# Expert products in turn: the second product of one expert position beside the first product of the next

## The chip, the cores and the metric

The kernel runs on one core of one Trainium2 chip. The metric is device time in microseconds (us) of one execution. Three timed runs of the kernel before took 490.77, 490.84 and 494.41 us, so the median is 490.84 us.

## The reference

A retention attention (4 batches, 8 heads, 768 positions, head width 64, blocks of 64) makes `x`, 3072 tokens of 512 numbers. Then a mixture of 8 experts is applied to it: each token goes to the one expert with the largest logit.

```
logits = x @ w_gate
e_idx = np.argmax(logits, axis=1)
gate_w = probs[np.arange(N), e_idx]
eom = 1.0 / (1.0 + np.exp(-(x @ w_output_gate)))
for e in range(E):
    mask = e_idx == e
    h = np.maximum(x[mask] @ w1[e], 0.0)
    ye = h @ w2[e]
    out[mask] = gate_w[mask, None] * eom[mask, e, None] * ye
```

`w1[e]` is 512x1024 and `w2[e]` 1024x512, all in 32-bit floating point. The change touches only the loop over the experts, which is the second half of the kernel's time.

## The kernel before

**Positions.** The experts are sorted by how many tokens chose them. Position 0 is the fullest. The capacity `CAP` of the positions is 448, 432, 416, 400, 400, 384, 368 and 368 tokens. Capacity in blocks of 128 rows (`KT`) is 4 for positions 0 to 4 and 3 for 5 to 7. Positions 1 to 4 are `TURNED`: their second product is computed with the output features on the partitions and turned back afterwards. The others, called rows positions here, compute it with the tokens on the partitions.

**One product is three matmuls.** Each 32-bit operand is split into a high and a low part of type fp32r, and `mm3` (L77 to L80) adds high by high (L78), high by low (L79) and low by high (L80) in one PSUM bank.

**The stages of a position.** The first product (`up`, matmuls to the tiles `ph`) runs over 8 feature groups `fc`, each with 4 inner steps, so 8 x 4 x 3 = 96 matmuls. After each `fc`, `up_act` takes the ReLU on ScalarE (`hhi`, L923) and the low part on VectorE (`hlo`, L924). Then the second product runs: for a turned position, `down` makes 4 output groups of 24 matmuls each (`py`), so 96; for a rows position, KT row blocks of 24 matmuls (`pyr`). In the kernel before, all of `up` of a position stands ahead of all of its second product, and that ahead of the next position.

**What runs beside it.** A weight piece of 1 MB is loaded on SyncE's queue (L128, L130) and split by quarters, high part on ScalarE (L143) and low part on VectorE (L152); two pieces of `w1` and two of `w2` per position, in three raw buffers. GpSimd (POOL) gathers the rows of `x` two positions ahead by indirect DMA (L792, 12 to 14 per position), VectorE transposes them (L883) and ScalarE and VectorE split them (L895, L896). After a turned second product, VectorE transposes the bank (`zt`, L985), scales it (`yo`, L991), and POOL scatters the rows to the output by indirect DMA (L1002, 13 or 14 per position). A rows position scales each block (L1063) and scatters it with one DMA (L1066). `down_banks` fills the unused columns of a bank with zeros (L940) where the capacity is no multiple of 32; that is so for positions 1, 3 and 4, and in the kernel before it stands in the middle of `up`.

**What sets the order.** Everything stands under a manual schedule: each engine runs its instructions in the order in which the program text issues them. The main loop of the kernel below fixes the order; buffers come round from pools (8 PSUM banks with the tag `bank`, 45 slots with the tag `slot`), where a new tile waits for the last use of the oldest one.

## Time and profile before

| | before |
|---|---|
| three timed runs | 490.77, 490.84, 494.41 us |
| the profiled execution's own time | 494.69 us |
| its span | 493.0 us |
| mean granted TensorE clock | 0.933 |
| TensorE (PE) busy | 438.5 us (89%) |
| VectorE (DVE) busy | 281.4 us (57%) |
| GpSimd (POOL) busy | 273.9 us (56%) |
| ScalarE (ACT) busy | 200.6 us (41%) |

Times inside the execution are counted from the start of the span. The positions follow the attention and the routing: the second product of position 1 starts at 209.22 us, the first product of position 2 at 228.79, and the last second product ends at 487.88. A PE that is busy is not a PE at its peak: matmuls overlap in the pipeline, so the time from one matmul's start to the next one's, the pitch, says more than the duration of one.

### The profile page before, as it was taken

To read this page: it belongs to the slowest core of one execution; us is meant where nothing else is said; L and a number is where in the kernel's file an instruction comes from. 1 tells how busy PE (TensorE), PEld (TensorE's weight loads), DVE (VectorE), ACT (ScalarE), POOL (GpSimd) and SP (SyncE) were. 2 spreads that over 40 slices of the span, in tenths; PEclk is the share of its full clock that TensorE was granted. 3 is DMA by queue.
4 is the path that set the end of the run, shared out by engine and by line. 5 is a ranking of instruction groups with operands and counts; after the bars stand their busy time and mean duration, and the time that the engine had idled before them with its cause. 6 is when DMAs were issued, how large, how long until landed. Compare 5 with 4: busy or idle time off the path is not lost.

```text
span 493.0 us, 10864 instructions
## 1 busy us (share of the span) xinstructions
PE 438.5 (89%) x4016; PEld 385.1 (78%) x4016; DVE 281.4 (57%) x791; ACT 200.6 (41%) x505; POOL 273.9 (56%) x323
## 2 busy tenths in 40 slices
PE   8999999978699989999549966998799869999995
PEld 5799888866597958889439953998599748898985
DVE  5677776727666266495039621957196248186531
ACT  3688787737332134270125201632171234073410
POOL 5587888676616777637731775076637735601002
PEclk9999999979889999999859995999889959999999
DMA  9999999975312929728105451555527245745001
GB/s 188 214 279 270 261 246 245 235 185 188 98 63 58 208 60 288 170 102 212 55 29 162 163 115 40 121 185 122 129 97 197 70 107 195 186 107 195 19 21 41
DMA packets 85512, 73.04 MB, mean 148 GB/s; under 512 B 58572, under 2 KB 64528, under 8 KB 85456
## 3 DMA queue, kind: packets, MB, share of 16 engines
q1 hardware_dynamic: 76192, 51.58, 41.0%
q0 software_dynamic: 9120, 20.73, 14.6%
q8 instruction: 33, 0.54, 0.5%
q14 instruction: 23, 0.19, 0.1%
q10 hardware_dynamic: 144, 0.00, 0.0%
HBM read 59.27 MB, written 13.41 MB: 147 GB/s over the span
## 4 chain that ended last, share of the span: by engine, by line
PE 78%; issue 9%; DVE 3%; DMA 3%; another core or an unknown queue 2%; SPq 2%; ACT 1%; POOL 0%; POOLq 0%; ACTq 0%; DVEq 0%
PE ph_None L80 9%; PE ph_None L79 9%; PE ph_None L78 9%; PE ps L393 5%; PE py L80 5%; PE py L78 5%; PE py L79 5%; PE pyr L79 4%; PE pyr L78 4%; PE pyr L80 4%; PE po L445 4%; PE po L481 3%; PE pk L341 2%; PE po L428 2%
## 5 line engine op out<-in xcount | busy, mean ns | idle before, releaser
L792 POOL DMA_INDIRECT xg<-x_d,rows x89 | 96.5, 1085 | 89.4 <-issue 35.8
L923 ACT ACTIVATE hhi<-ph_None 128x400 fp32r<-128x400 f32 (+4 forms) x56 | 28.1, 502 | 173.0 <-remote 85.5
L80 PE MATMUL ph_None<-xhi,wlo 128*128 128x400 f32 (+4 forms) x224 | 80.8, 361 | 16.9 <-issue 16.8
L78 PE MATMUL ph_None<-xhi,whi 128*128 128x400 f32 (+4 forms) x224 | 80.5, 359 | 9.3 <-issue 9.1
L79 PE MATMUL ph_None<-xlo,whi 128*128 128x400 f32 (+4 forms) x224 | 81.1, 362 | 6.9 <-issue 6.8
L152 DVE TENSOR_TENSOR wlo<-raw,whi 128x512 fp32r<-128x512 f32 x128 | 84.5, 683 | 3.2 <-ACT whi L143 2.7
L924 DVE SCALAR_TENSOR_TENSOR hlo<-ph_None,hhi 128x400 fp32r<-128x400 f32 (+4 forms) x56 | 31.4, 560 | 93.8 <-issue 64.3
L143 ACT CAST whi<-raw 128x512 fp32r<-128x512 f32 x128 | 74.5, 616 | 2.1 <-DMA raw<-in_moe_w_dram 2.1
L1002 POOL DMA_INDIRECT out_dram<-yo,outrow x53 | 53.3, 1006 | 18.9 <-issue 14.9
L78 PEld LDWEIGHTS ph_None<-xhi,whi 128*128 128x128 f32 x224 | 44.3, 198 | 18.6 <-issue 17.0
L80 PEld LDWEIGHTS ph_None<-xhi,wlo 128*128 128x128 f32 x224 | 44.7, 199 | 17.3 <-issue 16.9
L79 PEld LDWEIGHTS ph_None<-xlo,whi 128*128 128x128 f32 x224 | 44.4, 198 | 12.8 <-issue 12.4
L79 PE MATMUL py<-hlo,whi 128*128 128x400 f32 (+2 forms) x128 | 45.2, 353 | 0.1
L80 PE MATMUL py<-hhi,wlo 128*128 128x400 f32 (+2 forms) x128 | 45.1, 352 | 0.1
L78 PE MATMUL py<-hhi,whi 128*128 128x400 f32 (+2 forms) x128 | 45.1, 352 | 0.0
L403 DVE TENSOR_TENSOR at<-ps,decay 128x512 f32<-128x512 f32 x48 | 31.6, 685 | 23.4 <-PE ps L393 19.7
L1066 POOL DMA_INDIRECT out_dram<-yn,table x12 | 12.2, 1014 | 51.5 <-DVE yn L1063 28.8
L78 PE MATMUL pyr<-whi,hhi 128*128 128x512 f32 (+2 forms) x96 | 38.4, 400 | 1.2 <-ACT hhi L923 1.2
L79 PE MATMUL pyr<-wlo,hhi 128*128 128x512 f32 (+2 forms) x96 | 38.3, 399 | 0.9 <-DVE wlo L152 0.8
L80 PE MATMUL pyr<-whi,hlo 128*128 128x512 f32 (+2 forms) x96 | 38.1, 397 | 0.5 <-issue 0.5
L361 ACT COPY qT<-pq 64x256 f32<-64x256 f32 x88 | 34.4, 391 | 3.3 <-PE pq L341 2.5
L638 POOL DMA_INDIRECT tab_d<-rec,idx x24 | 24.9, 1037 | 17.1 <-issue 15.8
(182 smaller groups left out, 831.5 us busy)
## 6 DMA issues: line engine op xcount, KB each, us to landing
raw<-in_moe_w_dram SPq DMA_DIRECT2D x15, 1024.0 KB
raw<-in_moe_w_dram SPq DMA_DIRECT2D x24, 512.0 KB
qkv<-in_k_dram SPq DMA_DIRECT2D x20, 256.0 KB
qkv<-in_v_dram SPq DMA_DIRECT2D x20, 256.0 KB
qkv<-in_q_dram SPq DMA_DIRECT2D x38, 128.0 KB
x_d<-xn POOLq DMA_DIRECT2D x17, 256.0 KB
raw<-in_moe_w_dram SPq DMA_DIRECT2D x16, 128.0 KB
raw<-in_moe_w_dram POOLq DMA_DIRECT2D x4, 512.0 KB
```

What stands on the lines that cost most here:

```text
L78: nc.tensor.matmul(ps, a[0], b[0], start=first, stop=False)
L79: nc.tensor.matmul(ps, a[0], b[1], start=False, stop=False)
L80: nc.tensor.matmul(ps, a[1], b[0], start=False, stop=last)
L143: nc.scalar.copy(out=hi, in_=src)
L152: eng.tensor_tensor(out=lo, in0=src, in1=hi.bitcast(F32), op=ALU.subtract)
L361: nc.scalar.copy(out=view(qT[0][r]), in_=src)
L403: nc.vector.tensor_tensor(out=at, in0=ps.rearrange("p (g t) -> p g t", g=NPAIR), in1=dec[:, j], op=ALU.mult)
L638: nc.gpsimd.indirect_dma_start(out=tab_d, out_offset=bass.IndirectOffsetOnAxis(ap=idx, axis=0), in_=rec, in_offset=None, bounds_check=P * ...
L792: nc.gpsimd.indirect_dma_start(out=xg[(p, b // 4)][:, (b % 4) * P : (b % 4 + 1) * P], out_offset=None, in_=x_q, in_offset=bass.IndirectOff ...
L923: nc.scalar.activation(out=hi[:, r], in_=ph[:, r], func=AF.Relu)
L924: nc.vector.scalar_tensor_tensor(out=lo[:, r], in0=ph[:, r], scalar=0.0, in1=hi[:, r].bitcast(F32), op0=ALU.max, op1=ALU.subtract,)
L1002: nc.gpsimd.indirect_dma_start(out=out.rearrange("t (q f) -> (t q) f", q=4), out_offset=bass.IndirectOffsetOnAxis(ap=ogs[p][0][:, b : b + ...
```

## The change

The change is in the order of the instructions. The number of matmuls, of DMAs and of bytes is the same.

First, a class `Buffers` hands out banks and slots: the program says itself when a tile is given back (`free`), and the next `take` gets the one given back longest ago. 8 banks are held that way, 13 slots of 32-bit data and 32 of split parts. Second, from position 1 on the loop takes, for each position `p`, its second product in 8 steps, one `fc` each: 4 banks at once, 3 matmuls for each (12 matmuls, 9 in a rows position). Between two steps stand the 12 matmuls of one `fc` of the first product of position `p + 1`. All four banks of the second product are complete only after step 7, and are then turned together (`turn_bank`); scaling and scattering of them (`scale_rows`, `emit_turned`) move into the next turn of the loop, into its groups 0 and 1. Third, the gathers stand three positions ahead of `p`, behind the scatters, and the weight pieces are split in the order in which they are used now, in buffers of their own for each of the two products. Fourth, the zero fill of `down_banks` now stands at the start of a turn, ahead of step 0. Position 7 runs its second product alone.

In the order listings, line numbers are those of the kernel before (L78 to L80) or of the changed one (L101 to L103), and a tile bears the name that its buffer was first taken under: a bank named `ph_0` can hold a second product, and a slot named `xg` scaled rows.

TensorE at the start of the second product of position 1, before:

```order
L79 MATMUL ph_7_None<-xlo_3_3381,whi_3489 128x432
L80 MATMUL ph_7_None<-xhi_3_3380,wlo_3490 128x432
L78 MATMUL py_0_3638<-hhi_0_3549,whi_3553 128x432
L79 MATMUL py_0_3638<-hlo_0_3550,whi_3553 128x432
L80 MATMUL py_0_3638<-hhi_0_3549,wlo_3554 128x432
L78 MATMUL py_0_3638<-hhi_1_3572,whi_3553 128x432
L79 MATMUL py_0_3638<-hlo_1_3573,whi_3553 128x432
L80 MATMUL py_0_3638<-hhi_1_3572,wlo_3554 128x432
```

One bank takes the groups 0 to 7 of `h` in a row. TensorE at the end of step 1 of the same position in the changed kernel, with the first product of position 2 behind it:

```order
L102 MATMUL ph_2_None<-hlo_1_3610,whi_3554 128x432
L103 MATMUL ph_2_None<-hhi_1_3609,wlo_3555 128x432
L101 MATMUL ph_3_None<-hhi_1_3609,whi_3554 128x432
L102 MATMUL ph_3_None<-hlo_1_3610,whi_3554 128x432
L103 MATMUL ph_3_None<-hhi_1_3609,wlo_3555 128x432
L101 MATMUL ph_4_None<-xhi_0_3748,whi_3703 128x416
L102 MATMUL ph_4_None<-xlo_0_3749,whi_3703 128x416
L103 MATMUL ph_4_None<-xhi_0_3748,wlo_3704 128x416
L101 MATMUL ph_4_None<-xhi_1_3752,whi_3703 128x416
```

The rows with 432 columns are the second product of position 1, now with a new bank after every three matmuls; those with 416 columns are the first product of position 2.

VectorE around the zero fill of position 3, before (`hlo` is the low part of h, `wlo` that of a weight quarter):

```order
L924 SCALAR_TENSOR_TENSOR hlo_3_4552<-ph_3_None,hhi_3_4551 128x400
L152 TENSOR_TENSOR wlo_4476<-raw_4335,whi_4475 128x4x4x32
L940 MEMSET py_0_4560 128x16
L940 MEMSET py_1_4562 128x16
L940 MEMSET py_2_4564 128x16
L940 MEMSET py_3_4566 128x16
L924 SCALAR_TENSOR_TENSOR hlo_4_4582<-ph_4_None,hhi_4_4581 128x400
```

The fill stands behind group 3 of the first product, four groups ahead of its use. The same place in the changed kernel, from the turned banks of position 2 on (L1021 is the transpose of a bank, L922 the low part of x of position 4, into slots first named `hlo`):

```order
L1021 STREAM_TRANSPOSE xg_0_3888<-ph_1_None 128x416
L177 TENSOR_TENSOR wlo_4529<-raw_4417,whi_4528 128x512 x2
L922 TENSOR_TENSOR hlo_0_3848<-y_1_4455,hhi_0_3847 128x160
L922 TENSOR_TENSOR hlo_2_3966<-y_1_4455,hhi_2_3965 128x160
L950 SCALAR_TENSOR_TENSOR hlo_6_3778<-ph_6_None,hhi_6_3777 128x400
L177 TENSOR_TENSOR wlo_4529<-raw_4417,whi_4528 128x512 x2
L922 TENSOR_TENSOR hlo_3_4016<-y_1_4455,hhi_3_4015 128x160
L922 TENSOR_TENSOR hlo_1_3610<-y_1_4455,hhi_1_3609 128x160
L950 SCALAR_TENSOR_TENSOR hlo_7_3789<-ph_7_None,hhi_7_3788 128x400
L972 MEMSET ph_2_None 128x16
L972 MEMSET ph_3_None 128x16
L972 MEMSET ph_4_None 128x16
```

The fill now stands behind the low part of group 7, which is the last work of the turn, and its use is the next thing TensorE does.

POOL's indirect DMAs from the gather for position 4 on, before (a gather reads `x_d`, a scatter writes `out`):

```order
L792 DMA xg_0_4217<-x_d,rows_4212 128x128 x4
L792 DMA xg_1_4230<-x_d,rows_4212 128x128 x4
L792 DMA xg_2_4243<-x_d,rows_4212 128x128 x4
L792 DMA xg_3_4256<-x_d,rows_4212 128x128
L1002 DMA out_dram<-yo_0_4295,outrow_4041 12288x128 x4
L1002 DMA out_dram<-yo_1_4297,outrow_4041 12288x128 x4
L1002 DMA out_dram<-yo_2_4299,outrow_4041 12288x128 x4
L1002 DMA out_dram<-yo_3_4301,outrow_4041 12288x128
```

Here 13 gathers stand at the start of the second product of position 2 and its 13 scatters behind them. In the changed kernel, from the scatter of position 2 on:

```order
L1043 DMA out_dram<-xg_1_3635,outrow_4375 12288x128 x4
L1043 DMA out_dram<-xg_0_3622,outrow_4375 12288x128 x4
L1043 DMA out_dram<-yo_0_4203,outrow_4375 12288x128 x4
L1043 DMA out_dram<-yo_1_4205,outrow_4375 12288x128
L817 DMA yo_2_4207<-x_d,rows_4663 128x128 x4
L817 DMA yo_3_4209<-x_d,rows_4663 128x128 x4
L817 DMA xg_3_3927<-x_d,rows_4663 128x128 x4
```

The scatters of position 2 come first and the gathers for position 6 directly behind them, both issued in group 1 of the turn in which the second product of position 3 runs.

The diff, with the removed lines left out (they stand in the kernel above):

```diff
+    class Buffers:
+        def __init__(self, make):
+            self.make, self.count, self.back, self.held = make, None, [], []
+        def hold(self, count):
+            self.count = count
+        def take(self, name, newest=False):
+            if self.count is None:
+                return self.make(name)
+            if len(self.held) < self.count and not (newest and self.back):
+                self.held.append(self.make(name))
+                return self.held[-1]
+            return self.back.pop(-1 if newest else 0)
+        def free(self, t):
+            if any(t is h for h in self.held):
+                self.back.append(t)
+    def slots_of(dtype):
+        return Buffers(lambda name: pool.tile([P, 512], dtype, tag="slot", bufs=NSLOT, name=name))
+    banks = Buffers(lambda name: psum.tile([P, 512], F32, tag="bank", name=name))
+    slots, parts = slots_of(F32), slots_of(F32R)
+    bank, slot, part = banks.take, slots.take, parts.take
...
+            side = 0 if i == len(pieces) - 1 else pieces[i][1]
             wparts[pieces[i]] = (
...
+                wpool.tile([P, 4, 512], F32R, tag=f"whi{side}", bufs=2, name=f"whi_{i}"),
+                wpool.tile([P, 4, 512], F32R, tag=f"wlo{side}", bufs=2, name=f"wlo_{i}"),
             )
...
         nc.vector.transpose(ys[(p, i // 2)][:, 512 * (i % 2) : 512 * (i % 2) + w], xg[(p, i)][:, 0:w])
+        slots.free(xg[(p, i)])
...
+            hts[(p, fc)] = (part(f"hhi_{p}_{fc}"), part(f"hlo_{p}_{fc}"))
...
+        banks.free(ph)
...
+    def down_blocks(p):
+        return list(range(NKC if p in TURNED else KT[p]))
     def down_banks(p):
...
+        for j in down_blocks(p):
+            py = phs[(p, "y", j)] = bank(f"py_{p}_{j}")
+            if p in TURNED and CAP[p] < 32 * NB[p]:
                 nc.vector.memset(py[:, CAP[p] : 32 * NB[p]], 0.0)
...
+    def down(p, fc, js):
+        whi, wlo = wparts[(p, 1, fc // 4)]
+        hi, lo = hts[(p, fc)]
+        for j in js:
+            py = phs[(p, "y", j)]
+            if p in TURNED:
+                sl = slice(j * P, (j + 1) * P)
+                mm3(
+                    py[:, 0 : CAP[p]], (whi[:, fc % 4, sl], wlo[:, fc % 4, sl]),
+                    (hi[:, 0 : CAP[p]], lo[:, 0 : CAP[p]]), fc == 0, fc == NFC - 1,
+                )
+            else:
+                r = slice(j * P, min(j * P + P, CAP[p]))
+                mm3(
+                    py[0 : r.stop - r.start, :], (hi[:, r], lo[:, r]), (whi[:, fc % 4, :], wlo[:, fc % 4, :]),
+                    fc == 0, fc == NFC - 1,
+                )
...
+    zts = {}
+    def turn_bank(p, dc):
         py = phs.pop((p, "y", dc))
...
+        zt = zts[(p, dc)] = slot(f"zt_{p}_{dc}", newest=True)
+        nc.vector.transpose(zt[:, 0 : 32 * NB[p]], py[:, 0 : 32 * NB[p]])
+        banks.free(py)
+    def scale_rows(p, dc):
+        zt, nb = zts.pop((p, dc)), NB[p]
         for k in range(KT[p]):
             if dc == 0:
...
+                yts[(p, k)] = slot(f"yo_{p}_{k}")
             bs = slice(4 * k, min(4 * k + 4, nb))
             n = bs.stop - bs.start
             nc.vector.tensor_tensor(
...
+                out=yts[(p, k)].rearrange("p (b f) -> p b f", b=4)[:, 0:n, 32 * dc : 32 * dc + 32],
                 in0=zt.rearrange("p (b c) -> p b c", c=32)[:, bs],
                 in1=ogs[p][1][:, bs].unsqueeze(2).broadcast_to([P, n, 32]),
                 op=ALU.mult,
             )
+        slots.free(zt)
...
+        order = [4, 5, 6, 8, 7, 9]
+        for p in range(2, E):
+            order += [i for i in (4 * p + 2, 4 * p + 4, 4 * p + 3, 4 * p + 5) if i < len(pieces)]
+        done = [0]
+        def next_split(count):
+            for _ in range(count):
+                i, j = divmod(done[0], 4)
+                if i >= len(order):
+                    return
+                split_quarter(order[i], j)
+                if j == 3 and i + 2 < len(order):
+                    load_piece(order[i + 2], nc.gpsimd if i == 0 else nc.sync)
+                done[0] += 1
+        work = next_x(1)
+        for fc in range(NFC):
+            up(0, fc, 1)
+            if fc >= 4:
+                next_split(1)
+                for f in work[:2]:
+                    f()
+                work = work[2:]
+            if fc == 0:
+                load_rows(2)
+            if fc == 4:
+                row_index(2)
+                gather(2)
+        for j in range(2, KT[0]):
             for fc in range(NFC):
...
+                down_rows_mm(0, j, fc)
+            if j == 2:
+                for f in work:
                     f()
...
+                next_split(4)
+            emit_rows(0, j, phs.pop((0, "y", j)))
+        banks.hold(8)
+        slots.hold(NSLOT - 4 * NPAIR - 2 * NFC)
+        parts.hold(4 * NPAIR + 2 * NFC)
+        load_rows(3)
+        load_rows(4)
+        work = next_x(2)
+        for fc in range(NFC):
+            for kc in range(NKC):
+                up_mm(1, fc, None, kc)
+            if fc > 0:
+                up_act(1, fc - 1, None)
+            next_split(1)
+            if fc == 1:
+                out_index(1)
+            if fc == 2:
+                row_index(3)
+                gather(3)
+            for f in {5: work[0:2], 6: work[2:6], 7: work[6:7]}.get(fc, ()):
+                f()
+        up_act(1, NFC - 1, None)
+        rest = work[7:]
+        for p in range(1, E - 1):
+            nxt = p + 1
+            down_banks(p)
+            js = down_blocks(p)
+            x = next_x(p + 2)
+            last = p - 1
+            old = [lambda d=d: scale_rows(last, d) for d in range(NKC)] if last in TURNED else []
+            tasks = {i: [] for i in range(NFC)}
+            tasks[0] += old[0:2]
+            tasks[1] += old[2:4]
+            tasks[1].append(lambda: row_index(p + 3))
+            if last in TURNED:
+                tasks[1].append(lambda: emit_turned(last))
+            tasks[1].append(lambda: gather(p + 3))
+            tasks[6].append(lambda: load_rows(p + 4))
+            if nxt not in TURNED:
+                tasks[0].append(lambda: load_outs(nxt))
+            if p in TURNED and p > 1:
+                tasks[2].append(lambda: out_index(p))
+            if p == 1:
+                tasks[3].append(count_over)
+            tasks[3] += x[0:2]
+            tasks[4] += x[6:8] + x[2:3]
+            tasks[5] += x[3:6]
+            tasks[6] += x[8:10]
+            tasks[7] += x[10:12]
+            def step(fc):
+                down(p, fc, js)
+                for t in hts.pop((p, fc)):
+                    parts.free(t)
+            step(0)
+            for i in range(NFC):
+                if i < NFC - 1:
+                    step(i + 1)
+                if p == 1 and i == 0:
+                    for f in rest:
+                        f()
+                if i == NFC - 2 and p in TURNED:
+                    for d in range(NKC):
+                        turn_bank(p, d)
+                elif i == NFC - 2:
+                    for j in js:
+                        emit_rows(p, j, phs.pop((p, "y", j)))
+                for kc in range(NKC):
+                    up_mm(nxt, i, None, kc)
+                next_split(2)
+                for f in tasks[i]:
+                    f()
+                up_act(nxt, i, None)
+            for g in range(NPAIR):
+                for t in xts.pop((nxt, g)):
+                    parts.free(t)
+        p = E - 1
+        nc.gpsimd.drain()
+        for j in range(KT[p]):
+            if j == KT[p] - 1:
+                last_rows(p, j)
+                continue
+            for fc in range(NFC):
+                down_rows_mm(p, j, fc)
+            emit_rows(p, j, phs.pop((p, "y", j)))
```

111 lines of the change are left out of this document (9 added, 102 removed).

## The prediction

> **What bounds the kernel now.** I read the page's shares and its chain of waits first, then TensorE's waits, then the windows by stage, and last the instructions of TensorE and POOL one by one where a window came out too long. The page's share of TensorE and its chain:
>
> ```profile
> PE 438.5 (89%) x4016; PEld 385.1 (78%) x4016; DVE 281.4 (57%) x791; ACT 200.6 (41%) x505; POOL 273.9 (56%) x323
> ...
> PE 78%; issue 9%; DVE 3%; DMA 3%; another core or an unknown queue 2%; SPq 2%; ACT 1%; POOL 0%; POOLq 0%; ACTq 0%; DVEq 0%
> ```
>
> TensorE is the path, with 78% of the chain; another 9% is "issue", time for which the profile shows no releaser. The view of TensorE's waits says where:
>
> ```profile
> PE ph_None L80 <- issue: 16.8, 20, 1.6
> PE ph_None L78 <- issue: 9.1, 14, 1.6
> PE ph_None L79 <- issue: 6.8, 14, 1.6
> ```
>
> (Columns: total us, times, longest.) All of it is in the first products, 32.7 us in 48 waits. No such row exists for the second products of the turned positions. The windows by stage, cut where the tile changes; columns are length, then busy time and instructions of PE, PEld, DVE, ACT and POOL, granted clock, DMA share, GB/s:
>
> ```profile
> 209.22:228.79 19.57, 19.32 (x98) 17.98 (x96) 17.03 (x45) 9.27 (x22) 9.76 (x9) 1.00 0.40 134
> 228.79:264.07 35.28, 23.54 (x98) 20.25 (x96) 12.41 (x41) 6.98 (x14) 18.27 (x19) 0.76 0.37 90
> 264.07:282.15 18.08, 18.08 (x98) 17.98 (x96) 15.23 (x43) 7.42 (x18) 10.01 (x10) 1.00 0.47 154
> 282.15:315.68 33.53, 24.89 (x98) 20.02 (x97) 12.17 (x41) 7.50 (x16) 17.29 (x17) 0.75 0.37 90
> 315.68:332.96 17.28, 17.28 (x98) 17.28 (x97) 11.21 (x33) 6.80 (x16) 10.36 (x10) 1.00 0.57 172
> 332.96:358.88 25.92, 20.64 (x98) 18.13 (x98) 12.52 (x44) 6.26 (x13) 15.14 (x16) 0.92 0.51 120
> 377.45:403.41 25.96, 20.42 (x97) 17.66 (x97) 8.52 (x17) 6.00 (x13) 17.33 (x18) 0.85 0.52 124
> 420.99:438.74 17.75, 16.49 (x97) 16.01 (x96) 8.57 (x16) 6.50 (x14) 6.98 (x7) 1.00 0.56 135
> 455.16:471.16 16.00, 16.00 (x98) 16.00 (x97) 9.16 (x15) 6.90 (x14) 0.97 (x1) 1.00 0.05 14
> ```
>
> The rows are the second product of position 1, then first and second products of 2 and of 3, then the first products of 4 to 7. Each is 96 matmuls. Where nothing disturbs, 96 take 18.08 us at 416 columns (a pitch of 0.188), 17.28 at 400 and 16.00 at 368, so about 16.7 at 384 (16.00 x 384 / 368). The first products of positions 2 to 6 take longer by 35.28 - 18.08 = 17.20, 33.53 - 17.28 = 16.25, 25.92 - 17.28 = 8.64, 25.96 - 16.7 = 9.26 and 17.75 - 16.00 = 1.75: together 53.1 us. This is the sum that the change plays for.
>
> **What the stalls look like.** TensorE's instructions in the first product of position 2, and finer windows, in the same columns as above:
>
> ```profile
> 238.13 0.45 PE L78 MATMUL ph_None<-xhi,whi 128*128 128x416 f32 x1
> 239.55 0.35 PE L79 MATMUL ph_None<-xlo,whi 128*128 128x416 f32 x1 [0.97 <-issue]
> 240.97 0.35 PE L80 MATMUL ph_None<-xhi,wlo 128*128 128x416 f32 x1 [1.07 <-issue]
> ```
>
> ```profile
> 172.00:182.00 10.00, 8.87 (x40) 6.04 (x40) 5.42 (x12) 4.07 (x11) 7.54 (x8) 1.00 0.16 46
> 334.40:337.30 2.90, 1.61 (x7) 1.14 (x8) 2.62 (x7) 0.00 (x0) 1.01 (x1) 1.00 0.16 45
> 338.80:350.40 11.60, 11.44 (x64) 11.11 (x62) 6.47 (x29) 3.04 (x6) 9.07 (x9) 1.00 0.61 146
> 228.79:237.65 8.86, 8.86 (x49) 8.80 (x47) 2.68 (x7) 1.02 (x2) 6.72 (x8) 1.00 0.74 164
> 237.65:255.80 18.15, 6.41 (x16) 3.35 (x14) 2.42 (x12) 1.02 (x2) 11.55 (x12) 0.63 0.14 44
> 255.80:264.07 8.27, 8.27 (x36) 8.09 (x36) 7.31 (x22) 4.93 (x10) 0.00 (x0) 0.79 0.48 111
> ```
>
> A matmul that should follow after 0.19 us follows after 1.42, within one bank, with operands long there. The half clock is a result, since it is still 1.00 when the stalls begin, and costs its own part afterwards: 36 matmuls in 8.27 us, a pitch of 0.230. The common mark is POOL. Its rows:
>
> ```profile
> 186.65 1.08 POOL L792 DMA_INDIRECT xg<-x_d,rows  x1 [1.43 <-issue]
> ...
> 206.23 0.95 POOL L1066 DMA_INDIRECT out_dram<-yn,table  x1 [0.31 <-issue]
> ...
> 216.60 1.06 POOL L792 DMA_INDIRECT xg<-x_d,rows  x1 [9.42 <-issue]
> ...
> 251.57 0.98 POOL L1002 DMA_INDIRECT out_dram<-yo,outrow  x1 [0.30 <-issue]
> ...
> 269.39 1.05 POOL L792 DMA_INDIRECT xg<-x_d,rows  x1 [16.84 <-PE py L80]
> ...
> 338.76 1.03 POOL L1002 DMA_INDIRECT out_dram<-yo,outrow  x1 [3.07 <-DVE yo L991]
> ...
> 365.31 1.37 POOL L792 DMA_INDIRECT xg<-x_d,rows  x1 [9.87 <-DVE y L883]
> ...
> 398.98 0.98 POOL L1002 DMA_INDIRECT out_dram<-yo,outrow  x1 [0.30 <-issue]
> ```
>
> From 216.60 to 252.55 POOL issues 28 indirect DMAs, one each 1.3 us: 14 gathers, then 14 scatters. The stall begins at 237.65, 21 us into that run, and ends 3 us after it. From 365.31 to 399.96 it is the same; from 269.39 on 26 follow each other, some 34 us. Where a pause of 3.07 us parts the run, the scatters from 338.76 on go beside a dense TensorE for 11.6 us (64 matmuls in the window). What links POOL to TensorE's sequencer no view shows. I read the rows as: a run of indirect DMAs over some 20 us makes TensorE crawl for its remainder.
>
> **Part by part.** *The order of matmuls.* Their number and shapes stay, so dense time stays. Taking every loss of the first products off the profiled execution's own time gives 494.69 - 53.1 = 441.6 us.
>
> *Four banks open.* The second product needs 4 banks for a whole turn and the first one cycles through the rest. Up_act of a group has the 12 matmuls of the next step as cover, some 2.2 us, against one ReLU and one low part of 0.56 (row below). I take nothing; without cover it would be about 1 us a group.
>
> *The zero fill.* VectorE's groups from 205 us on:
>
> ```profile
> L152 DVE TENSOR_TENSOR wlo<-raw,whi 128x512 fp32r<-128x512 f32 x100 | 66.2, 683 | 0.5 <-ACT whi L143 0.5
> L924 DVE SCALAR_TENSOR_TENSOR hlo<-ph_None,hhi 128x400 fp32r<-128x400 f32 (+4 forms) x52 | 29.0, 557 | 92.2 <-issue 62.7 <-ACT hhi L923 29.4
> L896 DVE TENSOR_TENSOR xlo<-y,xhi 128x256 fp32r<-128x256 f32 (+2 forms) x48 | 15.2, 357 | 0.7 <-ACT xhi L895 0.7
> ...
> L985 DVE STREAM_TRANSPOSE zt<-py 128x416 f32<-128x416 f32 (+1 forms) x16 | 10.0, 622 | 18.4 <-PE py L80 13.1 <-PE ph_None L80 4.7 <-remote 0.5
> ...
> L940 DVE MEMSET py<- 128x16 f32 x8 | 0.2, 72 | 0.0
> ```
>
> At the start of positions 3 and 4, step 0 waits for the fill of its bank, and the fill stands on VectorE behind everything that begins when step 7 of the position before ends: 4 transposes (4 x 0.622), 4 weight parts (4 x 0.683), 4 parts of x (4 x 0.357), 2 low parts (2 x 0.557) and the fill (4 x 0.072), 8.0 us in all. TensorE has 24 matmuls of the first product for it, 24 x 0.18 = 4.3 us. It waits 3.7 us, twice. At position 1 there are no transposes; the last ReLU and low part and the fill come after TensorE's last matmul, some 1.2 us. Sum 8.6 us; its bounds are 0, should VectorE's overlap hide it, and twice that. Who waits behind it: TensorE's whole queue.
>
> *Scales, splits and loads.* The scaling moves one turn on and is waited for by POOL alone. Splits and weight loads keep their number per position; VectorE has 12 to 17 us of work in stages of 17 to 19 us dense, so they fit, though with little to spare. I take nothing.
>
> *POOL.* The gathers for position 3 no longer wait behind the first product of position 1: the gap of 9.42 us before 216.60 goes, and the gathers for position 4 follow. From 186.65 on 13 + 2 + 13 + 13 = 41 DMAs of 1.31 us stand in a row, 53.7 us. After that come 14 scatters and 12 gathers, then twice 13 and 12, and 13 scatters alone: 33.8, 32.5, 32.5 and 16.9 us, each in a turn of some 35 us, so parted by pauses of a few us. Past the 20 us mark lie 33.7 + 13.8 + 12.5 + 12.5 = 72.5 us, nearly all of it gathers now, since the scatters stand first in a run. What a us past the mark costs TensorE beside scatters: 17.20 / 16.0 = 1.08 in the first run, 9.26 / 14.7 = 0.63 in the one from 365.31. Beside gathers: in 334.40 to 337.30 7 matmuls took what 16 could have, 1.64 of 2.90 us, or 0.57; in 172 to 182 the idle time is 1.13 of 10.00, or 0.11. I take 0.4, nearer to the first, whose matmuls have the same shape: 29 us (8 to 41).
>
> *Sum.* 441.6 + 8.6 + 29 = 479.2 us for the profiled execution, which is 3.85 above the median of the runs; by the ratio 490.84 / 494.69 that is 475.5, say 476. With the ends of the gathers' price it is 455 to 487.
>
> **Rivals.** *The stall needs scatters late in a run.* Then nothing is left of it, as scatters now come first: 441.6 + 8.6 = 450.2, or 447 us. For it: 338.80 to 350.40, scatters after a pause and a dense TensorE. Against it: 334.40 to 337.30, a stall with gathers alone.
>
> *The stall goes with the scatters wherever they are.* All 53 of them remain: the loss of 53.1 stays, and the fill adds 0 to 8.6, 491 to 499 us. For it: the long stalls all lie in scatters. Against it: the same dense window.
>
> *Slower: the run's length decides, at the scatters' price.* The place is POOL's queue from 186.65 on; the 72.5 us past the mark cost 0.93 each (42.7 us lost in 45.7 us past the mark, the runs from 216.60, 269.39 and 365.31), 67 us: 441.6 + 8.6 + 67 = 517, or 513. It decides once a us of gathers costs more than (53.1 - 8.6) / 72.5 = 0.61. Against it: both gather rows are below that.
>
> *The clock drops at the bank changes.* If the granted clock fell as in 255.80 to 264.07 (pitch 0.230 for 0.188, 22% more) throughout the changed stages, their dense 245.9 - 53.1 = 192.8 us (209.22 to 455.16) would grow by 42, to 450.2 + 42 = 492, or 489 us. The Trainium skill, page "TensorE: Matmul & The Clock Gate", section "A second HAM failure mode: psum-queue depth-cycling", has such a case: cycling through PSUM banks left small idle gaps between groups of matmuls, and the clock swung between half and full. Against it here: the window from 455.16 changes banks every 12 matmuls with 16.00 of 16.00 us busy and the clock at 1.00; what a change every 3 does no row shows.
>
> **How the numbers follow.** About 1% can be told from no change. Forecast 0.36 (0.05 of it within 1%), no stall left 0.20, stall with the scatters 0.22 (0.12 within 1%, 0.10 slower), long runs 0.16, clock 0.06 (0.04 within 1%, 0.02 faster and slower). Faster 0.52, within 1% 0.21, slower 0.27. The range 445 to 506 leaves out most of the long runs and the lower end of the second case, some 0.2.
>
> **What would show it.** "Issue" in TensorE's waits below 20 us confirms the forecast; above 30 the third or fourth case holds; near 0 the second. Stalls should lie in POOL's gathers and not in scatters. A wait of 2 to 4 us on VectorE's fill should stand at the start of positions 3 and 4. POOL should have a run of over 45 us from about 187 on. The forecast is wrong if stalls start within 5 us of a run's first DMA, if they appear with POOL idle, or if TensorE waits for weight or x parts by more than 5 us in all.

## The result, and the profile after

The changed kernel takes 521.59 us (four runs, 521.34 to 526.49) where the kernel before takes 491.71 (490.77 to 494.41): a ratio of 1.062, with a 95% interval of 1.055 to 1.070. It is slower by some 30 us. The forecast was 476 us, faster than before, and the range 445 to 506. The profiled execution of the kernel before was one of its slower ones (494.69 us), so three or four microseconds between its profile and that of the changed kernel mean nothing.

The page of the changed kernel, its shares and its chain:

```profile
PE 446.8 (86%) x4016; PEld 390.4 (75%) x4016; DVE 279.3 (54%) x791; ACT 199.7 (38%) x505; POOL 275.2 (53%) x323
...
PE 64%; another core or an unknown queue 10%; DVE 7%; issue 7%; DMA 4%; ACT 2%; SPq 2%; POOL 2%; POOLq 0%; DVEq 0%
```

TensorE's share of the chain falls from 78 to 64%; VectorE rises from 3 to 7%, and "another core or an unknown queue" from 2 to 10%. TensorE's waits:

```profile
PE ph_None L101 <- issue: 22.8, 18, 8.8
PE ph_None L102 <- issue: 14.2, 21, 1.7
PE ph_None L103 <- issue: 11.8, 16, 2.3
PE ph_None L101 <- DVE ph_None L972: 4.7, 2, 2.8
```

48.8 us are named "issue", where before had 32.7. Below them stands the zero fill, 4.7 us in two waits, which before did not have. The windows of three turns (one turn: the second product of a position and the first product of the next), cut at the first gap between matmuls (columns as in the prediction):

```profile
278.14:293.75 15.61, 15.61 (x86) 15.56 (x85) 9.44 (x29) 4.90 (x10) 12.26 (x12) 1.00 0.68 183
293.75:315.33 21.58, 9.17 (x20) 5.09 (x20) 1.00 (x3) 0.00 (x0) 14.28 (x15) 0.57 0.14 43
336.05:352.85 16.80, 16.80 (x95) 16.80 (x94) 10.19 (x35) 4.91 (x10) 13.14 (x13) 1.00 0.61 168
352.85:372.04 19.19, 9.84 (x25) 5.61 (x24) 2.81 (x6) 2.44 (x6) 13.23 (x13) 0.64 0.46 102
389.92:406.31 16.39, 16.39 (x94) 16.23 (x94) 10.24 (x35) 4.86 (x10) 12.80 (x12) 1.00 0.63 173
406.31:426.31 20.00, 9.55 (x23) 5.37 (x22) 2.90 (x6) 2.66 (x7) 13.17 (x13) 0.58 0.40 96
```

Each first window begins with POOL's first scatter of a run. Three times TensorE is dense for 15.6 to 16.8 us and then crawls for 19 to 22 us, until some 3 us after the run's last DMA. The first 12 or 13 DMAs of a run, all scatters, pass without harm; nearly all of the stall lies beside the gathers behind them, and it is no milder than the one that stood beside scatters. Gathers alone are enough: a run of 13 gathers from 237.16 us on has a short stall from 251.74.

### The profile page after: what moved, and what is told of

It is laid out like the page before. It is cut to its first block, busy times and chain, and to the rows that moved or that the text cites. A ratio compares the mean times of both kernels' runs of the same rounds, so it can differ in the third digit from the quotient of the medians.

```text
span 519.7 us, 10851 instructions
## 1 busy us (share of the span) xinstructions
PE 446.8 (86%) x4016; PEld 390.4 (75%) x4016; DVE 279.3 (54%) x791; ACT 199.7 (38%) x505; POOL 275.2 (53%) x323
## 4 chain that ended last, share of the span: by engine, by line
PE 64%; another core or an unknown queue 10%; DVE 7%; issue 7%; DMA 4%; ACT 2%; SPq 2%; POOL 2%; POOLq 0%; DVEq 0%
PE ph_None L101 13%; PE ph_None L102 13%; PE ph_None L103 13%; PE ps L418 5%; PE po L470 4%; PE po L506 3%; PE po L453 2%; PE pk L366 2%; DVE wlo L177 2%; PE pq L483 2%; PE pq L366 2%; DMA xg<-x_d,rows 2%; ACT whi L168 1%; DVE hlo L950 1%
## 5 line engine op out<-in xcount | busy, mean ns | idle before, releaser
L101 PE MATMUL ph_None<-hhi,whi 128*128 128x400 f32 (+4 forms) x236 | 86.7, 368 | 21.3 <-issue 18.5
L103 PE MATMUL ph_None<-hhi,wlo 128*128 128x400 f32 (+4 forms) x236 | 87.2, 370 | 11.5 <-issue 11.5
L102 PE MATMUL ph_None<-hlo,whi 128*128 128x400 f32 (+4 forms) x236 | 86.7, 368 | 11.5 <-issue 11.5
L177 DVE TENSOR_TENSOR wlo<-raw,whi 128x512 fp32r<-128x512 f32 x128 | 82.8, 685 | 16.1 <-ACT whi L168 15.6
L168 ACT CAST whi<-raw 128x512 fp32r<-128x512 f32 x128 | 72.9, 618 | 17.3 <-DMA raw<-in_moe_w_dram 17.2
L1043 POOL DMA_INDIRECT out_dram<-xg,outrow x30 | 31.7, 1058 | 70.6 <-DVE xg L1031 62.4
L101 PEld LDWEIGHTS ph_None<-hhi,whi 128*128 128x128 f32 x236 | 48.1, 204 | 25.2 <-issue 24.1
L103 PEld LDWEIGHTS ph_None<-hhi,wlo 128*128 128x128 f32 x236 | 48.2, 204 | 16.9 <-issue 16.4
L102 PEld LDWEIGHTS ph_None<-hlo,whi 128*128 128x128 f32 x236 | 48.1, 204 | 16.9 <-issue 16.0
L101 PE MATMUL ph_None<-xhi,whi 128*128 128x432 f32 (+4 forms) x116 | 42.2, 363 | 6.3 <-issue 4.3
L102 PE MATMUL ph_None<-xlo,whi 128*128 128x432 f32 (+4 forms) x116 | 42.6, 367 | 2.4 <-issue 2.4
L103 PE MATMUL ph_None<-xhi,wlo 128*128 128x432 f32 (+4 forms) x116 | 42.0, 362 | 0.4 <-issue 0.4
L101 PEld LDWEIGHTS ph_None<-xhi,whi 128*128 128x128 f32 x116 | 23.2, 200 | 7.5 <-issue 4.8
```

Source lines behind the costliest of these rows:

```text
L101: nc.tensor.matmul(ps, a[0], b[0], start=first, stop=False)
L102: nc.tensor.matmul(ps, a[0], b[1], start=False, stop=False)
L103: nc.tensor.matmul(ps, a[1], b[0], start=False, stop=last)
L168: nc.scalar.copy(out=hi, in_=src)
L177: eng.tensor_tensor(out=lo, in0=src, in1=hi.bitcast(F32), op=ALU.subtract)
L1043: nc.gpsimd.indirect_dma_start(out=out.rearrange("t (q f) -> (t q) f", q=4), out_offset=bass.IndirectOffsetOnAxis(ap=ogs[p][0][:, b : b + ...
```

## The experiments

What is stated after the result: the *long-run theory* (TensorE crawls once an unbroken run of indirect DMAs, one each 1.3 us, is 16 to 20 us old) against theories that blame the gaps between weight loads, the scatters as such, or the alternation of the two products. Beside that, one thing of the first windows was not explained: TensorE waits 8.8 us at once ahead of position 1.

The runs fell on several chips of the same kind, and that turned out to matter more than any edit. On some the kernel before takes 426 to 428 us ("quiet" below), on others 495 to 497, like the 492 above ("stalling"). Each result is given with the kernel before on the same chip. Every chip was met only once, so what belongs to the chip and what to the moment is not told apart.

### The rows form, the scatters left out, and the weight piece

Rows form, in the old order (`b_rows`) and in the new one (`a_rows`, with `load_outs(1)` added for position 1):

```diff
-    TURNED = [p for p in range(1, E) if KT[p] == 4]
+    TURNED = []
```

> The kernel before, with every second product in the rows form: 4 scatters of whole rows per position where positions 1 to 4 had 13 or 14 of quarter rows. TensorE's dense time grows, since 96 matmuls of 512 columns take some 21.8 us (pitch 0.227) where they took 18.9, 18.1, 17.3 and 17.3: +15.6 us. Long-run theory (TensorE crawls from some 16 to 20 us into an unbroken run of indirect DMAs until about 3 us after it): runs of 13 gathers and 4 scatters are 20 to 22 us long, as ahead of the first product of position 6, which lost 1.75 us; so the 51.3 us lost in the first products of positions 2 to 5 fall to about 7, and the time is near 491 - 51 + 7 + 16 = 463 us. Load-gap theory (TensorE crawls when indirect DMAs have run for 3 us without a weight load beside them): the gathers meet the same gaps, the stalls start about as early and end earlier, loss halved, near 480 us. If neither, and the stalls belong to the first products as such: near 506 us.

> The changed kernel with every second product in the rows form. Per turn 13 gathers from group 1 on and 4 scatters in group 6, so no run over 17 to 22 us; dense time +15.6 us, no zero fill. Long-run theory: the stalls from 293.75, 352.85 and 406.31 us of the changed kernel's profile (21.6, 19.2 and 20.0 us long) go, and the two waits for the fill (2.3 and 3.1): 521.6 - 55 - 5 + 16 = 478 us. Load-gap theory: some 5 to 10 us of stall stay per turn, near 505 us. If the stalls come from switching banks or from the alternation itself: 532 us or more.

Scatters of quarter rows left out of the changed kernel (`a_no_scatter`):

```diff
     def emit_turned(p):
-        for b in range(NB[p]):
-            scatter(
...
         for k in range(KT[p]):
             slots.free(yts[(p, k)])
```

> The changed kernel; left out: the scatters of positions 1 to 4, whose rows of the output aren't written. POOL has runs of 12 or 13 gathers alone, 16 to 17 us. Long-run theory: the long stalls of three turns go, 521.6 - 55 = 467 us. Load-gap theory: gathers without a load beside them still stall TensorE, over 490 us. Alternation theory: no change, 521 us.

The weight piece on SyncE's queue (`a_piece_sp`):

```diff
-                    load_piece(order[i + 2], nc.gpsimd if i == 0 else nc.sync)
+                    load_piece(order[i + 2])
```

> The changed kernel with one edit: the weight piece that POOL's queue issues at 202.16 us, behind 13 gathers (184.38 before the change), goes to SyncE's queue instead. If that piece is what keeps ScalarE idle 17.2 us on a raw piece and with it VectorE idle until 208.90 us, TensorE's wait of 8.8 us ahead of position 1 and its slow first product of position 1 go: -9 to -15 us, 507 to 513 us. If the wait there is another stall beside POOL's gathers: no change, 521 us.

Measured on a quiet chip, before at 426.66 us: `b_rows` 444.3 (ratio 1.039, 1.032 to 1.046), `a_rows` 457.0 (1.069, 1.062 to 1.076), `a_no_scatter` 449.4 in one run, `a_piece_sp` 438.9 (1.025, 1.018 to 1.033). None of the levels was foreseen, since before itself was 65 us faster here; the theories on the stalls can't be told apart where there are none. The rows form costs 17.6 us where 15.6 had been worked out from the pitch.

### Both kernels again, and the fill

Before and after unchanged (`before_again`, `after_again`), and the changed kernel with the piece on SyncE's queue and the fill behind the transposes (`a_piece_fill`):

```diff
-            down_banks(p)
+            if p == 1 or p not in TURNED:
+                down_banks(p)
...
                     for d in range(NKC):
                         turn_bank(p, d)
+                    if nxt in TURNED:
+                        down_banks(nxt, True)
```

> The kernel before once more, to have its trace where it takes some 427 us and not 491. Chip theory (the stalls named issue are a state of the chip and not of the program: they don't occur on this chip whatever POOL does): no wait named issue in the first products, their 96 matmuls in 18.1, 17.3, 17.3 and 16.7 us; 427 us. Long-run theory: stalls 16 to 20 us into POOL's runs are still there and 491 us comes back.

> The changed kernel once more. If the loss against the kernel before is the change's own (late weight piece 9 to 15 us, fill and slots 8 us) and the stalls are the same in both kernels, the ratio is as it was, 1.05 to 1.07: near 451 us where before takes 427, and 521 where it takes 491. If stalls of POOL's runs made the loss, the ratio is within 1.02 where there are no stalls.

> The changed kernel with the weight piece on SyncE's queue and, for positions 3 and 4, the zero fill directly behind the four transposes of the turn before (the fill takes the banks just given back). Without the fill's wait, if that is the price: 4 to 8 us less than with the piece alone, some 431 us where before takes 427. If the waits only move (to the slots that POOL's scatters give back late): within 2 us of the piece alone, 437 to 439.

Measured on a quiet chip, before at 425.96: `after_again` 454.2 (1.064, 1.060 to 1.068), `a_piece_fill` 433.0 (1.014, 1.009 to 1.019); the profiled execution of `before_again` took 429.83. Both `again` runs came out near what was foreseen for a chip without stalls (427 and 451 us), and so did the 4 to 8 us for the fill (433.0 here, 438.9 with the piece alone on another quiet chip). The changed kernel loses the same 6% with and without stalls. Where it loses them is told by two stages, the first product of position 1 (first four rows) and all that follows up to the last second product (last four); in each group before, changed, `before_again`, `after_again`:

```profile
189.23:209.22 19.99, 19.34 (x98) 17.99 (x96) 9.63 (x33) 5.37 (x11) 14.06 (x13) 1.00 0.87 214
188.20:223.69 35.49, 23.23 (x96) 19.55 (x97) 19.57 (x58) 11.74 (x27) 21.20 (x21) 0.83 0.52 148
179.62:200.68 21.06, 20.73 (x97) 19.57 (x98) 16.85 (x49) 10.68 (x23) 15.79 (x14) 0.92 0.80 189
177.62:213.25 35.63, 19.26 (x96) 18.01 (x97) 19.56 (x58) 11.71 (x27) 21.14 (x21) 0.84 0.58 157
209.22:487.88 278.66, 245.95 (x1201) 222.03 (x1199) 150.73 (x394) 88.10 (x198) 129.87 (x124) 0.91 0.42 118
223.69:514.76 291.07, 251.28 (x1200) 226.17 (x1200) 142.38 (x377) 83.94 (x188) 124.15 (x118) 0.88 0.40 111
200.68:422.91 222.23, 222.23 (x1201) 213.09 (x1199) 151.74 (x389) 86.62 (x192) 135.69 (x125) 1.00 0.55 149
213.25:448.06 234.81, 228.38 (x1200) 217.99 (x1200) 142.95 (x377) 84.47 (x188) 127.29 (x118) 0.97 0.51 138
```

The change lengthens the first product of position 1 by 15.5 us on the stalling chip and by 14.6 on the quiet one, and the rest by 12.4 and 12.6. On the quiet chip 6.4 of the 12.6 us are two waits for the zero fill; what else is in them is not shown. The stalling chip lengthens the rest by 56.4 us before and by 56.3 after: taken together, the stalls were moved and not shortened.

Two windows of `before_again`, from the first matmuls of position 1 to the last second product, and over POOL's longest run:

```profile
180.94:422.91 241.97, 241.97 (x1295) 231.97 (x1293) 167.32 (x431) 95.98 (x211) 151.29 (x139) 0.99 0.57 152
204.90:369.20 164.30, 164.30 (x889) 160.66 (x888) 120.99 (x328) 66.81 (x148) 128.62 (x118) 1.00 0.63 169
```

POOL issues 118 DMAs in one unbroken run of 164 us and TensorE is busy for 164.30 of 164.30 us. So a long run alone need not stall anything; on this chip the kernel before has no loss that the change could win back. In the changed kernel there (`after_again`), the waits of TensorE and of ScalarE, and POOL around the weight piece:

```profile
PE ph_None L101 <- DVE ph_None L972: 22.8, 3, 16.4
```

```profile
ACT whi L168 <- DMA raw<-in_moe_w_dram: 17.4, 1, 17.4
```

```profile
190.54 1.01 POOL L817 DMA_INDIRECT xg<-x_d,rows  x1 [0.30 <-issue]
191.54 0.83 POOL L153 DMA_DIRECT2D raw<-in_moe_w_dram  x1
192.68 1.03 POOL L1100 DMA_INDIRECT out_dram<-yn,table  x1 [0.30 <-issue]
```

and the same piece in `before_again`:

```profile
177.61 0.84 POOL L130 DMA_DIRECT2D raw<-in_moe_w_dram  x1
...
180.75 1.08 POOL L792 DMA_INDIRECT xg<-x_d,rows  x1 [2.30 <-issue]
```

The piece is issued at 177.61 before and at 191.54 after: the gather for position 2 now stands ahead of it in POOL's queue. ScalarE waits 17.4 us for it, in order, with every ReLU of position 1 behind; VectorE's low parts and the fill come late in turn, and TensorE stops for 16.4 us ahead of the second product of position 1. The wait is put down to the fill, which is merely the last in that line. In the first profile of the changed kernel, too, ScalarE waits 17.2 us for this piece ahead of TensorE's 8.8 us that were not explained. Taking the piece away from there brings the ratio from 1.064 to 1.025, 16 us, which fits the 14.6 us of the stage above; moving the fill brings it to 1.014, another 5. The intervals of those last two ratios touch, but TensorE's waits for the fill fall with it, from 7.8 us in all to 2.6.

In `a_piece_sp` the longest wait for the fill, 4.9 us, has a part that was not in the prediction's sum:

```profile
308.83 0.62 DVE L1021 STREAM_TRANSPOSE yo<-ph_None 128x416 f32<-128x416 f32 x1 [3.66 <-DMA out_dram<-yo,outrow]
```

The fourth transpose waits 3.66 us for a slot that a scatter has not yet read, because POOL is behind.

### The gather back behind the piece

```diff
-            if fc == 4:
-                row_index(2)
-                gather(2)
+        row_index(2)
+        gather(2)
         for j in range(2, KT[0]):
```

This is `a_gather_back`. `a_gather_fill` adds the early fills, with `down_banks(1)` after group 3 of position 1's first product. `b_gather_early` is the kernel before with `row_index(2)` and `gather(2)` in group 4 of position 0.

> The changed kernel with one edit: the gather for position 2 stands behind the first product of position 0 again, so behind the weight piece that POOL's queue issues. Late-piece theory: ScalarE's wait of 17 us on that piece and TensorE's wait of 9 to 16 us ahead of position 1 go, and the piece no longer comes so early that it meets position 0's gathers: 454 - 18 = 436 us where before takes 426, ratio 1.02 to 1.03. If the wait ahead of position 1 has another cause: 450 to 454.

> The same, and the zero fills early: for position 1 after group 3 of its first product, as in the kernel before, for 3 and 4 directly behind the transposes. With both own losses of the change gone TensorE is dense from position 1 on, as it is in the kernel before on this chip: ratio 1.000 to 1.008, 426 to 429 us. If the alternation itself costs (bank changes, splits late): 432 us or more. Where stalls named issue occur, the same difference of some 27 us to the changed kernel.

> The kernel before with one part of the change alone: the gather for position 2 in group 4 of position 0's first product, ahead of the weight piece in POOL's queue. Late-piece theory: the piece is issued some 17 us late, ScalarE and VectorE wait for it, and TensorE stops ahead of the second product of position 1: +10 to +16 us, 436 to 442 us. If only the alternation makes that piece critical: within 3 us of before.

Measured on a stalling chip, before at 495.26: 528.9 (1.068, 1.058 to 1.078), 521.3 (1.052, 1.042 to 1.062) and 500.5 (493.4 to 504.8, too spread to tell from before). The two edits that help on a quiet chip hardly do here. In `b_gather_early` the piece is late too: POOL issues it at 201.25 us behind 13 gathers, ScalarE waits 14.3 us for it, and the first product of position 1 takes 30.7 us, against 20.0 in the first profile of before. So the old order needs that piece in time as well; what it costs in the whole stays open, since stalls cover it. The same kernel once more with two that shorten POOL's runs:

> The changed kernel with the gather for position 2 behind the weight piece and the zero fills early, once more. Where no wait named issue occurs (before near 426 us): 426 to 430 us, ratio 1.000 to 1.010, if the late piece and the fill were all that the change lost; 433 or more if the alternation has a price of its own. Where they occur (before near 491 to 495 us): 1.05 again.

> The kernel before with every second product in the rows form, once more. Where stalls occur: the long-run theory gives 491 - 51 + 7 + 16 = 463 us against 491 (ratio 0.94); if stalls come with POOL's gathers alone too, 490 and more. Where none occur: ratio 1.04 again.

`b_pause`:

```diff
             if not rows:
+                for _ in range(24):
+                    nc.gpsimd.memset(pause, 0.0)
                 emit_turned(p)
```

> The kernel before with 24 fills of a scratch tile on POOL (some 5 us) between the gathers and the scatters of positions 1 to 4; work is added, none left out. Long-run theory, where stalls occur: the runs of 35 us part into 17 and 17, each stall shrinks from 17 us to 3 to 6, 491 - 35 = 456 us. If POOL being busy, and not its DMAs, makes TensorE crawl: no gain or a loss, 491 to 500. Where none occur: 0 to 8 us slower, as POOL is nearly full there.

Measured on a stalling chip, before at 496.77: `a_gather_fill_2` 524.2 (1.054, 1.039 to 1.069), `b_rows_2` 456.2 (0.921, 0.911 to 0.931), `b_pause` 478.0, 485.2, 493.5 and 493.8 in four runs, too spread for a ratio, where 456 had been foreseen. TensorE's waits in `a_gather_fill_2`, and the stretch up to a stall with the stall itself:

```profile
PE ph_None L101 <- issue: 10.8, 13, 1.8
PE py L101 <- issue: 10.0, 11, 2.3
PE ph_None L103 <- issue: 9.1, 9, 1.8
PE py L103 <- issue: 8.5, 9, 1.7
```

```profile
191.50:209.83 18.33, 18.33 (x86) 17.48 (x86) 11.89 (x41) 6.42 (x13) 14.37 (x14) 0.91 0.65 174
209.83:232.17 22.34, 8.27 (x18) 4.23 (x17) 2.42 (x4) 1.55 (x4) 14.51 (x15) 0.63 0.20 55
```

A run of 26 gathers and 2 scatters of whole rows stalls TensorE as the mixed ones do, 18 us after its start, and second products (`py`) stall like first ones. The rows form has 16 or 17 DMAs in a run; its windows:

```profile
213.57:235.33 21.76, 21.76 (x102) 17.33 (x101) 8.79 (x17) 4.13 (x10) 16.88 (x17) 1.00 0.70 202
235.33:238.05 2.72, 1.51 (x6) 0.68 (x6) 0.00 (x0) 0.00 (x0) 0.76 (x1) 1.00 0.34 122
```

The stall begins in the last microsecond of the run, 22 us after its start, and lasts 2.7 us: 456 us beside 497, near the 463 of the long-run theory. The edit takes away the scatters of quarter rows together with the length, so by itself it doesn't show which of the two mattered. This is the fastest version on a stalling chip; on a quiet one it is 4% slower than before. `b_pause` fits only in part: the pause is 6.3 us and the 14 scatters behind the first one meet no stall, but POOL falls behind, the next gathers follow the scatters without a pause, and a stall begins 27 us into that run.

### What is left of the alternation, and the rate

> The changed kernel with the gather behind the weight piece and the fills early, a third time, for a chip where before takes some 426 us: 426 to 430 us there if the late piece and the fill are all of the change's own loss, 433 or more if the alternation has a price of its own. Where before takes 491 or more: 1.05 again, since its second products then stall too.

> The changed order with every second product in the rows form, the gather for position 2 behind the weight piece, the one for position 3 in group 0 of the first turn and the later ones in group 4, so that no run of POOL's DMAs is over some 22 us. Where stalls occur, by the long-run theory: as good as the rows form in the old order, 450 to 458 against 491 to 497. Where none occur: 426 + 16 = 442. If the alternation has a price of its own: 5 us or more above these.

`a_rows_spread` is the changed order with `TURNED = []` and `load_outs(1)` as in `a_rows`, `gather(2)` moved as above, `gather(3)` in group 0 of the first turn and the later gathers in group 4:

```diff
-            tasks[1].append(lambda: row_index(p + 3))
+            if p == 1:
+                tasks[0].append(lambda: row_index(3))
+                tasks[0].append(lambda: gather(3))
+            tasks[4].append(lambda: row_index(p + 3))
...
-            tasks[1].append(lambda: gather(p + 3))
+            tasks[4].append(lambda: gather(p + 3))
```

Measured on a quiet chip, before at 428.15: 433.5 (1.013, 1.006 to 1.020) and 448.0 (1.051, 1.041 to 1.060). The changed order without its two losses, over the same work as the window of `before_again` above, and one whole turn of it:

```profile
183.26:427.39 244.13, 242.95 (x1295) 232.26 (x1293) 162.54 (x431) 95.62 (x211) 151.41 (x139) 0.99 0.55 148
```

```profile
208.02:243.90 35.88, 35.88 (x189) 35.17 (x188) 24.88 (x64) 14.52 (x32) 24.14 (x24) 1.00 0.62 150
```

Both results lie beyond the mark that was set for a price of the alternation itself (433 or more, and 5 us above 442). The windows say where the time goes. 244.13 us stand against 241.97. Of the 2.2 us more, 1.2 are one wait for the slot and the fill ahead of 311.49. Ahead of the window TensorE waits for parts of x of position 1, longer than in `before_again` (second row):

```profile
PE ph_None L101 <- ACT xhi L921: 4.5, 1, 4.5
PE ph_None L78 <- ACT xhi L895: 1.3, 1, 1.3
```

These 2.2 and 3.2 us make up the 5 us of the ratio. So by these two profiles the new order costs 5 us, most of it ahead of position 1; the alternation itself, from position 1 on, costs 1 or 2 us at most and wins nothing on a quiet chip. `a_rows_spread` came out 6 us above what was expected; its one wait of that size is this same 4.5.

The changed kernel without scatters once more (`a_no_scatter_3`), and a spaced version of the kernel before (`b_spaced`, with two fills ahead of each gather and of each scatter of quarter rows):

```diff
+    def space():
+        for _ in range(2):
+            nc.gpsimd.memset(beat, 0.0)
...
+            space()
             nc.gpsimd.indirect_dma_start(
```

> The changed kernel; left out: the scatters of positions 1 to 4, whose rows of the output aren't written. Where stalls occur: long-run theory, no stall over 4 us beside the gathers of the turns, which are 16 to 17 us long, so near 466 us; if gathers alone stall TensorE from their start, 490 or more. Where none occur: 449 again.

> The kernel before with two fills of a scratch tile on POOL ahead of each gather and each scatter of quarter rows; work is added, none left out. A DMA then comes each 1.6 to 1.75 us and not each 1.3. Where stalls occur: if the rate of POOL's DMAs makes them, they go, and POOL's 26 DMAs of some 44 us bound a position: 426 + 4 x 9 = 462 us. If the length of the run makes them, runs are longer (45 us and joined) and the loss grows: 510 to 540. Where none occur: POOL bounds positions 2 to 5, 450 to 465 us.

Both landed on a quiet chip, before at 426.19: 450.7 us (449.1 in another such run, `a_no_scatter_2`, before at 428.15), and 509.9 (1.200, 1.193 to 1.207). So the kernel without those scatters was not tried where stalls occur; that stalls need none of them is told by the runs of gathers in the changed kernel and in `a_gather_fill_2` above. `b_spaced` was foreseen at 450 to 465 us on a quiet chip, with a DMA each 1.6 to 1.75 us. A DMA came each 2.0 us, and the waits moved to POOL's transfers:

```profile
DVE y L890 <- DMA xg<-x_d,rows: 62.3, 14, 7.0
DVE yo L998 <- DMA out_dram<-yo,outrow: 45.5, 7, 7.8
```

0.7 us more for each of the 115 DMAs from position 3's gather on (62 gathers, 53 scatters) make 81 us, and the kernel is 84 us slower. Hardly any of it is hidden: 26 DMAs of 1.3 us are 34 us, and a dense position on TensorE is 36 (35.88 above). By this estimate POOL is within 2 us of being the bound of the turned positions.

## Why the prediction was wrong, point by point

- *The sum it played for.* The 53.1 us of stalls were read rightly off the trace, but taken for something that this program does by itself. It doesn't: `before_again` runs the same instructions, with a longer run on POOL, without one. Where they occur, both kernels lose the same to them: 491.71 - 425.96 = 66 us before, 521.59 - 454.23 = 67 after, from medians on different chips; 56 us each from the second product of position 1 on, by the windows above.
- *Part by part, "scales, splits and loads ... I take nothing".* This is the step that failed on the change itself, a term put at nothing because the number of loads stays. The gather for position 2 was followed into POOL's run, but not past the one thing that stands behind it in that queue, a weight piece. It measured 15.5 us in the first product of position 1 of the forecast's own comparison, and 16 by the ratios (1.064 to 1.025): more than half of the loss.
- *The zero fill,* 8.6 us with bounds 0 and 17: in `a_piece_sp` TensorE waits for it 7.8 us, and 5 us went with the fill moved. That the sum fits is luck in part: 1.2, 3.7 and 3.7 were added up, and the waits were 1.4, 1.4 and 4.9, the last of them made of a late slot, which was not foreseen. In the changed kernel of the first comparison the two waits were 1.95 and 2.76.
- *POOL, "I take 0.4".* This is the other step that failed. A us past the mark beside gathers was priced from two weak rows, 0.57 and 0.11. On the chip of the first comparison the stalls beside gathers were as deep as those beside scatters: 20 matmuls in the 21.58 us from 293.75. The three stalls shown there take 60.8 us for 68 matmuls that need some 12, so 48 us, in runs with 41 us past the mark: 1.2 for each. So nothing of the 53.1 us was won where 24 were forecast. With both steps set right the forecast's own sum comes out: 441.6 + 8.6 + 15.5 + 53.1 = 518.8 us, against 521.34 in the profiled execution. The rival "the run's length decides, at the scatters' price" gave 513 us and was nearest, with a chance of 0.16; its point of decision, 0.61 per us, was passed. It held for the stalls only on the chips that stall, it too lacked the late piece, and it counted a run from 187 us on that didn't come, so part of its nearness is luck.
- *The mark and the pause.* The runs counted were a little off (13 gathers and 14 scatters from 216.60, not 14 and 14). What matters more: a pause of 3.07 us was read as the end of a run, from a window that closes at 350.40 with TensorE dense. The next 7 us of the same run are a stall, 12 us after the pause:

```profile
350.43:357.58 7.15, 3.72 (x10) 2.35 (x11) 0.91 (x2) 1.01 (x2) 3.92 (x4) 0.81 0.69 160
```

So a pause of a few us is not enough for a run to start anew. `b_gather_early` shows it again: behind pauses of 1.2, 2.8 and 3.1 us stalls begin 2, 11 and 12 us into the run.
- *The run from 187 on,* 41 DMAs in a row, did not come: gather 3 waited for VectorE, which waited for the late piece, and the run broke there. Where the piece is in time, it does come in part (28 DMAs from 191.48 in `a_gather_fill_2`) and costs a stall of 22 us. That is how the corrected kernel can be no better than the changed one on a stalling chip: it takes 521 and 524 us on two of these and 433 on quiet ones, so it loses some 90 us there, where the kernel before loses 66 to 70.
- *Rivals that fell.* Stalls bound to scatters: they moved to the gathers. No stall left: wrong where before stalls. The clock: the turn from 208.02 us of `a_gather_fill_3` changes banks every 3 matmuls in its steps of the second product, at a granted clock of 1.00 with no idle time. The Trainium skill, page "TensorE: Matmul & The Clock Gate", section "A second HAM failure mode: psum-queue depth-cycling", describes a clock that swings between half and full where cycling through PSUM banks leaves frequent small idle times between groups of matmuls; this turn has none of those, so no run here puts that case to the test.

What stays open is the cause of the stalls. Every long one lies beside a run of POOL's indirect DMAs, and something that differs from chip to chip, or from moment to moment, decides whether it comes; no view names it. The length of the run is not the whole of it: in the loop over the experts on stalling chips, stalls began 13 to 27 us into runs that follow a pause of 5 us or more, and in `b_rows_2` six runs of 20 to 22.5 us met 2.7 us of stall at the most.

## What to carry to other kernels

When a step is moved ahead in an engine's queue, list what else stands in that queue behind its new place, DMAs of other purposes included; one load issued 14 us late cost almost twice the 8.6 us that had been worked out with care. Before a stall without a releaser is put into a sum as a gain, see whether the same program shows it on another chip. And where an engine off the critical path is taken up for 34 of 36 us, count its work per position first: it has no room for anything that the new order asks of it.

## What the runs showed of the hardware that was not expected

The same program took 426 us on some chips and 491 to 497 on others. The page has two signs of it: TensorE's waits named "issue", and what ends ScalarE's waits ahead of its ReLUs, "remote" (a releaser that the trace doesn't hold) in place of TensorE; the profile of before and that of `before_again`:

```profile
L923 ACT ACTIVATE hhi<-ph_None 128x400 fp32r<-128x400 f32 (+4 forms) x56 | 28.1, 502 | 173.0 <-remote 85.5
L923 ACT ACTIVATE hhi<-ph_None 128x400 fp32r<-128x400 f32 (+4 forms) x56 | 28.0, 501 | 120.1 <-PE ph_None L80 120.1
```

So on a stalling chip not only TensorE stands still. In `a_gather_back` ScalarE's instructions in the stretch beside POOL's run of gathers:

```profile
216.19 0.53 ACT L949 ACTIVATE hhi<-ph_None 128x432 fp32r<-128x432 f32 x1 [11.11 <-remote]
...
227.49 0.53 ACT L949 ACTIVATE hhi<-ph_None 128x432 fp32r<-128x432 f32 x1 [9.04 <-remote]
...
228.42 0.53 ACT L949 ACTIVATE hhi<-ph_None 128x432 fp32r<-128x432 f32 x1
```

and TensorE's last matmul ahead of them and its next one:

```profile
207.93 0.36 PE L103 MATMUL ph_None<-xhi,wlo 128*128 128x432 f32 x1
230.59 0.70 PE L101 MATMUL ph_None<-hhi,whi 128*128 128x432 f32 x1 [22.31 <-DVE ph_None L972]
```

TensorE's first product had ended by 208.3 us, and the ReLUs that read its last three groups started 8, 19 and 20 us later. What released the first two of them is not in the trace.
